# Twelve chunks of a linear attention and a gated feed-forward on one core: d_ff tiles of 512 tokens behind the attention, and filler matmuls in TensorE's planned waits

## The chip, the cores and the metric

The kernel runs on one core of one Trainium2 chip. The metric is the device time of one execution in microseconds. Lower is better.

## The reference

```python
def _attn_ref(r, k, v, w, a, b):            # B=4, H=8, S=768, D=40
    state = zeros(B, H, D, D)
    for t in range(S):
        y[:, :, t] = einsum('bhd,bhde->bhe', rt, state)
        Sa = einsum('bhde,bhe->bhd', state, at)
        state = state * wt[:, :, None, :] - einsum('bhd,bhe->bhde', Sa, bt) + einsum('bhd,bhe->bhde', vt, kt)
def _moe_ref(x, w_a, w_b, w_out):           # x: 3072 x 320, d_ff = 1536
    return ((x @ w_a) * (x @ w_b)) @ w_out
```

The attention's output, with batch and time as 3072 rows and the heads side by side as 320 columns, is the feed-forward's input.

## The kernel before

**Attention.** The 768 steps are cut into 12 chunks of 64 steps (`NS` = 12, `C` = 64). A pair of chunk and batch is numbered q, 48 in all. For each q `prep` scans the decay on VectorE, scales k, a and b, and forms masked 64x64 score blocks on TensorE (`pssc`, `psn`). Per chunk, `lanes` inverts the triangular 32x32 blocks of all heads: the masked blocks go by DMA to DRAM (`nb_d`), come back as one row per block (`N`), 62 small VectorE operations that wait for one another solve them (`Yt`, `psl`), and the results go out (`ts_d`) and back (`TT`) by DMA. `main` then runs the chain of q on TensorE with ScalarE or VectorE between the steps: `psr`, `psu`, `psut`/`psuu`, `psg`, `psy`, `psyt`; `self_state` adds `pss` and `psst`. Each of these ten steps takes one of the four PSUM banks of the attention by `at_take` and gives it back by `at_give`. `values` loads `UV`, `others` loads `rvt`, both on SyncE's queue.

**Feed-forward.** `xform` makes of a chunk's output the operand `xk` (256 tokens; high and low parts of the numbers stand as separate rows, so that 8 products of the list `KT` give one sum). A `Unit` is one tile of 128 d_ff columns for one chunk: 16 matmuls with 256 moving columns into one bank `ab` (two such banks), ScalarE copies one half out, VectorE multiplies it with the other, ScalarE rounds (`gh`), GpSimd takes the rest (`gl`), and 6 matmuls with 320 moving columns add into two banks `po`. There are 12 d_ff tiles and 12 chunks, so 144 units. The first five tiles (`F1`; fewer for the first two chunks, `FIRST`) run among the attention's steps as their chunk comes out, and their sum is kept in DRAM (`po_d`), as is `xk` (`xk_d`). Later tiles come two at a time (`groups`): the first group for chunks 0 and 1 still among the attention, all the rest behind it. A unit that is the last of its job adds `po` into `acc` on VectorE (two operations).

**Order.** All work is written as generators that yield `(engine, inputs, claim, condition)`. `Order.run` keeps a modelled time for each engine and takes, again and again, the step that could start first, `claim` being added to delay it. The program order on each engine is the order so found; the model is used only there. Its numbers are constants: `HOP` and `SPARE` are added to an operand that comes from another engine (`ready`), `LAND` and `PER_KB` price a DMA, and for TensorE it models a clock that halves when the last window of 3.413 us was streamed for less than 0.47 (`issue`). `NWAY`, `LATER`, `WAY`, `SPB`, `AHEAD` delay or permit steps (`after`, `lanes`, `late`). Nearly every DMA is issued by SyncE, in this order.

All instructions are recorded under one line (L178, `Issue.__getattr__`), so the profile is read by tiles.

Of the kernel before, what the change touches and what calls it, by code (L numbers as in the profile page):

```python
# [20 lines left out]
B = 4  # L21
H = 8
D = 40
C = 64
# [13 lines left out]
NI = 2  # L38
NL = 12
WAY = 0.5  # L40
LATER = 2.0
NWAY = 2
URG = 0.05
NEAR = 0.05
FIRST = (2, 3)
AHEAD = 4
SPB = 1
RAW = 2

LIMIT = 2.0 ** 8  # L50


PACE = 42.0
SPARE = 0.4
HOP = 0.1
LAND = 2.1
PER_KB = 0.0046
WINDOW = 3.413

# [8 lines left out]
class Order:  # L68
# [13 lines left out]

    def keys(self, x):
        name = x.name if isinstance(x.name, str) else str(x.name)
        if name.startswith("TT"):
            if any(step == C and n > 1 for step, n in x.ap[1:]):
                return [(name, b) for b in range(B)]
            return [(name, x.offset % (B * H * C) // C % B)]
        return [name]
# [8 lines left out]
    def issue(self, e, op, outs, ins, cost, delay, streamed=0.0):  # L98
        t = self.now[e]
        for x in ins:  # L100
            for k in self.keys(x):
                w, by = self.wrote.get(k, 0.0), self.by.get(k)
                t = max(t, w + (HOP if by != e else 0.0))
        for x in outs:
            for k in self.keys(x):
                if self.by.get(k) != e:
                    t = max(t, self.wrote.get(k, 0.0))
                t = max(t, self.read.get(k, (0.0, e))[0] if self.read.get(k, (0.0, e))[1] != e else 0.0)
        if e in self.port and op not in ("memset", "affine_select") and (e == "gpsimd" or sum(not str(x.name).startswith(("ps", "ab", "po")) for x in ins) > 1):

            t = max(t, self.port["gpsimd" if e == "vector" else "vector"])
            self.port[e] = t + cost
        if e == "tensor":
            w = int(t // WINDOW)
            if w > self.window:
                self.slow = w > self.window + 1 or self.busy < 0.47
                self.window, self.busy = w, 0.0
            self.busy += streamed / WINDOW
            if self.slow:
                cost += streamed  # L120
        elif e == "sync":
# [32 lines left out]
    def run(self):  # L154
        while self.parts:
            best = None
            for p in self.parts:
                e, deps, claim, may = p[1]
                if may is not None and not may():
                    continue  # L160
                t = max([self.now[e]] + [self.ready(x, e) for x in deps])
                t += claim(t) if callable(claim) else claim
                if best is None or t < best[0]:
                    best = (t, p)
            self.step(best[1])


class Issue:
# [18 lines left out]

    def cost(self, op, out, ins, kw):
        n = free(out)
        if self.name == "tensor":  # L190
# [17 lines left out]
        return 0.48, PER_KB * out.shape[0] * n * 4 / 1024  # L208


def token_by_token(tc, p, ps_at, pin, rv, done):
# [79 lines left out]
def wkv_moe(ctx, tc, pin, rv, vn, wa, wb, wo, out):  # L291
# [61 lines left out]
    nb1_d = [dram.tile([B * H, HB, HB], F32, name=f"nb1_d{n}") for n in range(NS)]  # L353
    ts_d = [dram.tile([2, B * H, HB, HB], F32, name=f"ts_d{n}") for n in range(NS)]


    def decode(raw, rows, ncol, dst_hi, dst_lo, claim):

# [77 lines left out]
    class Unit:  # L436
# [8 lines left out]
        def whole(self):  # L445
# [3 lines left out]
            Unit.open += 1  # L449
            Unit.turn.append(self)  # L450
            ab = order.tile(psab, [P, 2, 256], F32, tag="ab", name=f"ab{self.name}", bufs=2)
            for j in range(2):
                for i, (kw, kx) in enumerate(KT):
                    mul(ab[:, j, :], wt[:, j, kw, :], self.xk[:, kx, :], i == 0, i == 7)
                if j == 0:
                    yield "tensor", [], self.claim, None
# [35 lines left out]
            self.ended = True  # L492

        by = "scalar"


    wp = ctx.enter_context(tc.tile_pool(name="wp", bufs=1))
# [60 lines left out]
    def of_batch(x, b):  # L558
# [1 line left out]


    done = types.SimpleNamespace(
        i=0, scan=0, mix=0, free=0, prep=0, lanes=0, merge=0, loads=0, values=0, mask=0, main=0, y=0, state=0, x=0, moe=0, later=0, at=4, tmp=True)

    spare, held = {f"at{i}": None for i in range(4)}, {}

    def at_take(name):

        done.at -= 1
        tag = min(spare, key=lambda x: spare[x] or 0.0)  # L570
        del spare[tag]
        x = order.tile(psa, [P, 512], F32, tag=tag, name=name, bufs=1)
        held[str(x.name)] = tag
        return x

    def at_give(*tiles):
# [88 lines left out]
    def lanes(n):  # L665
        urgent, near = after(URG, n), after(NEAR, n)

        def blocks(hs_of):
            for p0, _, hs in HALVES:
                for j, nb in enumerate((nb0_d[n], nb1_d[n])):  # L670
                    sl = slice(j * HB, (j + 1) * HB)
                    nc.sync.dma_start(
                        out=nb[hs_of(hs)].rearrange("h s t -> s h t"),
                        in_=TT[n % 3][p0 + j * HB:p0 + (j + 1) * HB, hs_of(hs), sl])

# [5 lines left out]
        W = order.tile(pp, [P, 144], F32, tag="Yt", name="Yt", bufs=1)  # L681
        yield "sync", [nb0_d[n], nb1_d[n]], 0.0, None
        for p in range(2):
            nc.sync.dma_start(out=N[p * 64:p * 64 + 32], in_=nb0_d[n])
            nc.sync.dma_start(out=N[p * 64 + 32:p * 64 + 64], in_=nb1_d[n])
# [15 lines left out]
        Y = N[:, 0:HB // 2]  # L701
        nc.scalar.copy(out=Y.rearrange("p i t -> p (i t)"), in_=ps)
        at_give(ps)
        yield "sync", [Y], 0.0, None
        for p in range(2):
            nc.sync.dma_start(
                out=ts_d[n].rearrange("j h (i p) t -> p (j h) i t", p=2)[p], in_=Y[p * 64:(p + 1) * 64])
        done.lanes += 1

# [38 lines left out]

    def values(q):
        n, b = divmod(q, B)  # L750
        yield "sync", [], 0.0, lambda: done.values == q and (q or done.mask) and done.state > q - NU and done.scan > min(q + 2, NS * B - 1)
        done.values += 1
        for p0, hs, _ in HALVES:
            nc.sync.dma_start(out=UV[q % NU][C - p0:2 * C - p0, hs, :], in_=vn[n, b][:, hs])
# [145 lines left out]
    def xform(n):  # L900
        yield "scalar", [], 0.0, lambda: done.y == B * (n + 1) and done.moe >= n - 1
        x = xT_t.pop(n).rearrange("p g b t -> p g (b t)")
        xk = order.tile(mp, [PK, 6, B * C], F32R, tag="xk", name="xk", bufs=2)
        yield from expand(x, xk, nc.gpsimd)
        done.x += 1
        xks[n] = xk
# [1 line left out]
            yield "sync", [xk], 0.05, None  # L908
            nc.sync.dma_start(out=xk_d[n], in_=xk.bitcast(F32))

    acc = {}
    ready_w = set()
    ws1 = [weight_tiles(wp, i) for i in range(F1)]
    sets = [ws1[0:FG], ws1[FG:2 * FG]]
# [21 lines left out]
            return (out[n].rearrange("f p d -> p f d"), acc[n]) if last else None  # L936
        return f

    lp, xk2 = [None], {}

    def all_units():

        def job(n, kk):
            now = FIRST[n] if n < len(FIRST) else F1
            fs = range(now) if kk < 0 else [*range(now, F1), *groups[0]] if kk == 0 else groups[kk]
            last = kk == len(groups) - 1
            for i, f in enumerate(fs):
                yield n, kk, f, i == 0, i == len(fs) - 1, fin1(n) if kk < 0 else fin2(n, last)

        for n in range(NS - 1):  # L950
# [1 line left out]
        for n in range(NE):  # L952
            yield from job(n, 0)
        yield from job(NS - 1, -1)
        for n in (NS - 2, *range(NE, NS - 2), NS - 1):
            yield from job(n, 0)
        for kk in range(1, len(groups)):
            for n in range(NS):
                yield from job(n, kk)

    def moe():
        came = {}
        left = [NS * len(g) for g in groups]
        left[0] += sum(F1 - now for now in FIRST)
        for n, kk, f, first, last, fin in all_units():
            def x_there():
                return n in xks if kk < 0 or n >= NS - 2 else n in xk2
            claim = 0.06
# [31 lines left out]
            ready_w.add(f)  # L1000

    def load_x(pool, n):
        xk2[n] = order.tile(pool, [PK, 6, B * C], F32R, tag=f"xk2_{n}", name=f"xk2_{n}", bufs=1)
        nc.sync.dma_start(out=xk2[n].bitcast(F32), in_=xk_d[n])

    def load_acc(n):
# [162 lines left out]
```

## Time and profile before

| what | value |
|---|---|
| median of 3 runs | 1002.53 us (998.47 to 1003.49) |
| the profiled execution | 997.55 us |
| its span, first to last instruction | 995.8 us |
| TensorE busy, matmuls | 883.7 us (89%) |
| VectorE, ScalarE, GpSimd busy | 601.4, 450.0, 307.6 us |
| mean granted TensorE clock | 0.882 of full |

Tiles name the work: `ab` and `po` are feed-forward, names that begin with `ps` are steps of the attention, `N`, `Yt` and `psl` belong to `lanes`. PE is TensorE's matmul row, SPq the issuing SyncE. In a row of a timeline the columns are start, duration, engine, operation and how many were merged, with the idle time before it in brackets. `PEclk` is the granted clock. In a table of stretches each row has the length, then each engine's busy time with its count of instructions, then clock, DMA share and GB/s.

### The profile page before, as it was taken

What the parts mean: (1) busy time and instruction counts of PE and PEld (TensorE: products, weight loads), DVE (VectorE), ACT (ScalarE), POOL (GpSimd) and SP (SyncE); (2) the same over time, 40 slices, a digit from 0 to 9 for tenths busy, and PEclk for the clock granted to TensorE, in tenths of its full rate; (3) what the DMA queues carried; (4) which work ended last, traced back from release to release, by engine and by line L of the source; (5) the groups of instructions that cost most, each with busy time, mean ns of one, the idle gap of its engine ahead of it and who ended that gap; (6) DMA issues with size and microseconds to landing.
All of it is one profiled execution on the core that took longest, in us unless ns stands there. A gap on an engine that the chain in (4) does not pass through costs nothing.

```text
span 995.8 us, 23157 instructions
## 1 busy us (share of the span) xinstructions
PE 883.7 (89%) x8894; PEld 805.2 (81%) x8894; DVE 601.4 (60%) x1626; ACT 450.0 (45%) x1401; POOL 307.6 (31%) x443
## 2 busy tenths in 40 slices
PE   3146988689897789999999999999999999999997
PEld 3145877678787678888888888788899999999996
DVE  5777465877587847685858584724514648733343
ACT  4153454344555354655555656454533434422221
POOL 2230242323224232323322322213434636622222
PEclk9555677657697669999999999999999999999999
DMA  5452546535647245726555556346469402100013
GB/s 146 98 99 45 119 116 149 124 80 101 157 96 185 32 99 134 151 64 152 134 113 136 114 128 120 87 98 159 122 164 221 98 14 65 32 1 2 1 53 110
DMA packets 132945, 102.53 MB, mean 103 GB/s; under 512 B 86659, under 2 KB 118595, under 8 KB 132827
## 3 DMA queue, kind: packets, MB, share of 16 engines
q1 hardware_dynamic: 132827, 100.98, 43.3%
q8 instruction: 72, 1.18, 0.5%
q14 instruction: 46, 0.38, 0.1%
HBM read 77.03 MB, written 21.94 MB: 99 GB/s over the span
## 4 chain that ended last, share of the span: by engine, by line
PE 63%; DVE 17%; issue 5%; DMA 5%; ACT 4%; POOL 3%; SPq 2%; POOLq 0%; DVEq 0%; ACTq 0%
PE ab L178 23%; PE po L178 11%; PE psr L178 5%; DVE psl L178 5%; DVE Yt L178 4%; PE psg L178 4%; PE pss L178 4%; PE psy L178 3%; PE pssc L178 3%; PE psu L178 3%; SPq L178 2%; DMA N<-nb_d 2%; PE psyt L178 1%; ACT Abd L178 1%; PE psst L178 1%
## 5 line engine op out<-in xcount | busy, mean ns | idle before, releaser
L178 PE MATMUL ab<-xk,wt 120*128 120x256 f32 x2304 | 313.1, 290 | 9.5 <-DMA wt<-wt 3.3
L178 PEld LDWEIGHTS ab<-xk,wt 120*128 120x128 f32 x2304 | 295.6, 195 | 13.3 <-DMA wt<-wt 3.5
L178 POOL TENSOR_TENSOR gl<-asb,gh 128x256 fp32r<-128x256 f32 x144 | 110.9, 772 | 267.2 <-ACT gh L178 266.9
L178 PE MATMUL po<-wo,gh 128*128 128x320 f32 x576 | 157.6, 322 | 10.3 <-ACT gh L178 10.3
L178 DVE TENSOR_TENSOR asb<-ab,asb 128x256 f32<-128x256 f32 x144 | 60.7, 421 | 144.6 <-ACT asb L178 144.2
L178 ACT COPY asb<-ab 128x256 f32<-128x256 f32 x144 | 53.5, 372 | 147.0 <-PE ab L178 146.5
L178 PEld LDWEIGHTS po<-wo,gh 128*128 128x128 f32 x576 | 105.1, 193 | 12.9 <-ACT gh L178 11.7
L178 DVE TENSOR_TENSOR Yt<-psl,N 128x126 f32<-128x126 f32 (+22 forms) x372 | 94.2, 253 | 28.6 <-DMA N<-nb_d 17.3
L178 DVE TENSOR_TENSOR psl<-psl,Yt 128x126 f32<-128x126 f32 (+22 forms) x372 | 97.2, 261 | 11.6
L178 PE MATMUL po<-wo,gl 128*128 128x320 f32 x288 | 93.5, 325 | 5.1 <-POOL gl L178 4.8
L178 PE MATMUL pssc<-Abd,BK 120*128 120x192 f32 (+1 forms) x288 | 68.3, 389 | 30.7 <-ACT Abd L178 18.1
L178 ACT CAST gh<-asb 128x256 fp32r<-128x256 f32 x144 | 58.4, 406 | 75.5 <-DVE asb L178 71.1
L178 PEld LDWEIGHTS pssc<-Abd,BK 120*128 120x128 f32 x288 | 61.8, 247 | 33.3 <-ACT Abd L178 32.5
L178 POOL TENSOR_TENSOR pe<-Pc,rp 120x192 f32<-120x192 f32 x44 | 25.2, 573 | 167.7 <-DVE rp L178 149.5
L178 POOL TENSOR_TENSOR ST<-tmp,pcm 120x360 f32<-120x360 f32 x40 | 34.1, 852 | 100.4 <-DVE tmp L178 100.3
L178 PEld LDWEIGHTS po<-wo,gl 128*128 128x128 f32 x288 | 55.7, 193 | 10.3 <-POOL gl L178 9.7
L178 ACT ACTIVATE Abd<-A,m 120x192 f32<-120x192 f32 x144 | 54.8, 447 | 13.6 <-POOL A L178 11.8
L178 PE MATMUL psg<-rvt 120*128 120x192 f32 (+1 forms) x288 | 58.4, 350 | 0.9 <-DVE tmp L178 0.9
L178 DVE TENSOR_TENSOR acc<-po,acc 128x320 f32<-128x320 f32 x96 | 44.2, 490 | 20.6 <-PE po L178 20.6
L178 PEld LDWEIGHTS psg<-rvt 120*128 120x128 f32 x288 | 53.2, 217 | 2.1 <-DVE tmp L178 1.3
L178 PE MATMUL psr<-UV,TT 64*64 64x40 f32 x768 | 53.6, 254 | 0.5 <-ACT TT L178 0.5
L178 PEld LDWEIGHTS psr<-UV,TT 64*64 64x64 f32 x768 | 42.0, 159 | 14.4 <-issue 8.9
(101 smaller groups left out, 1429.3 us busy)
## 6 DMA issues: line engine op xcount, KB each, us to landing
rvt<-in_rv_dram SPq DMA_DIRECT2D x48, 450.0 KB
I<-in_pin_dram SPq DMA_DIRECT2D x46, 361.9 KB
xk_d<-xk SPq DMA_DIRECT2D x11, 720.0 KB
xk<-xk_d SPq DMA_DIRECT2D x10, 720.0 KB
N<-nb_d SPq DMA_DIRECT2D x48, 128.0 KB
wraw<-in_wa_dram SPq DMA_DIRECT2D x12, 360.0 KB
wraw<-in_wb_dram SPq DMA_DIRECT2D x12, 360.0 KB
wraw<-in_wo_dram SPq DMA_DIRECT2D x12, 320.0 KB
```

The costliest lines, as they stand in the source:

```text
L178: r = fn(*args, **kwargs)
```

## The change

Six things change together.

1. `Pair`: behind the attention (`done.y` and `done.state` complete) one d_ff tile runs for two chunks at once: 16 matmuls with 512 moving columns into two banks, one per half, then one operation each of ScalarE, VectorE, ScalarE and GpSimd over 512 columns, then 12 matmuls with 320 columns into four `po` banks, two of them taken from the attention's four. The last pair of a job adds four banks into two `acc` tiles and issues its two output DMAs after that. Pairs are formed of chunks (2,3) to (8,9) in the first later group and of all twelve chunks in the other groups. For this, `xk` of even and odd chunks lie side by side (`xkr`, `pairs`).
2. `warm`: before an attention step takes its bank, and before a unit takes its `ab` bank, the planner compares the start of the step that it has chosen with the time at which TensorE and the bank are free. If the wait is at least `GAP` (0.8 us), matmuls of the identity with itself (float32, 128 columns) are issued into that bank until no more than `MARGIN` (0.9 us) is left. The step's first matmul overwrites them. Nothing is added from the twelfth finished chunk on (`WARM`).
3. The planner's constants: `SPARE` 0.4 to 1.0, `LAND` 2.1 to 2.4, `NWAY` 2 to 1, `LATER` 2.0 to 1.5, `AHEAD` 4 to 3, `SPB` 1 to 2.
4. `values` waits until the first chunk's `N` loads have been issued (`done.blocks`), with a claim of 0.2 (`VC`). `others` follows `values`, so the `rvt` loads move behind them as well.
5. For the first chunk (`TSQ` = 1) the two `ts_d` writes are issued by ScalarE in place of SyncE. `TWOQ` and `NLQ` are 0 and do nothing.
6. The model of DMA issue covers ScalarE's queue too, and `run` passes the chosen step's start and engine on.

```diff
-LATER = 2.0
-NWAY = 2
+LATER = 1.5
+NWAY = 1
...
-AHEAD = 4
-SPB = 1
+AHEAD = 3
+SPB = 2
+GAP = 0.8
+MARGIN = 0.9
+TWOQ = 0
+TSQ = 1
+NLQ = 0
+VC = 0.2
+WARM = 12
...
-SPARE = 0.4
+SPARE = 1.0
-LAND = 2.1
+LAND = 2.4
...
+    def warm(ps):
+        if order.turn != "tensor" or done.x >= WARM:
+            return
+        t = max(order.now["tensor"], order.wrote.get(order.keys(ps)[0], 0.0))
+        if order.start - t < GAP:
+            return
+        while order.start - order.now["tensor"] > MARGIN:
+            mul(ps[:, 0:P], ident, ident)
...
             ab = order.tile(psab, [P, 2, 256], F32, tag="ab", name=f"ab{self.name}", bufs=2)
+            warm(ab.rearrange("p j t -> p (j t)"))
...
+    class Pair(Unit):
...
+        def whole(self):
+            wt, wot = self.w
+            yield "tensor", [self.xk, wt], self.claim, lambda: Unit.open < 3 and (
+                done.at + Unit.ab_free - 2 * (len(Unit.po or ()) < 4) >= 2)
...
+            ab = [self.take(f"{self.name}_{j}") for j in range(2)]
+            for j in range(2):
+                for i, (kw, kx) in enumerate(KT):
+                    mul(ab[j][0].rearrange("p (c t) -> p c t", c=2), wt[:, j, kw, :], self.xk[:, :, kx, :], i == 0, i == 7)
...
+            nc.scalar.copy(out=g, in_=ab[0][0])
...
+            nc.vector.tensor_mul(out=g, in0=ab[1][0], in1=g)
...
+            nc.scalar.copy(out=gh, in_=g)
...
+            nc.gpsimd.tensor_sub(out=gl, in0=g, in1=gh.bitcast(F32))
...
+            for hf in range(4):
+                sl = slice(hf * P, (hf + 1) * P)
+                po = Unit.po[hf][:, :DM]
+                mul(po, gh[:, sl], wot[:, 0, :], self.is_first, False)
+                mul(po, gl[:, sl], wot[:, 0, :], False, False)
+                mul(po, gh[:, sl], wot[:, 1, :], False, self.is_last)
...
         x = order.tile(psa, [P, 512], F32, tag=tag, name=name, bufs=1)
         held[str(x.name)] = tag
+        warm(x)
...
-        yield "sync", [Y], 0.0, None
+        eng = nc.scalar if n < TSQ else nc.sync
+        yield "scalar" if n < TSQ else "sync", [Y], 0.0, None
         for p in range(2):
-            nc.sync.dma_start(
+            eng.dma_start(
...
-        yield "sync", [], 0.0, lambda: done.values == q and (q or done.mask) and done.state > q - NU and done.scan > min(q + 2, NS * B - 1)
+        yield "sync", [], VC, lambda: done.values == q and done.blocks and done.state > q - NU and done.scan > min(q + 2, NS * B - 1)
...
-        for n in (NS - 2, *range(NE, NS - 2), NS - 1):
-            yield from job(n, 0)
+        yield from job(NS - 2, 0)
+        for n in range(NE, NS - 2, 2):
+            yield from job((n, n + 1), 0)
+        yield from job(NS - 1, 0)
         for kk in range(1, len(groups)):
-            for n in range(NS):
-                yield from job(n, kk)
+            for n in range(0, NS, 2):
+                yield from job((n, n + 1), kk)
```

More of the change, by code (lines that the diff above doesn't have):

```diff
@@ L84, in keys @@
         name = x.name if isinstance(x.name, str) else str(x.name)
+        if name.startswith("xkr"):
+            return [(name, x.offset % (12 * B * C) // (6 * B * C))] if len(x.shape) < 4 else [(name, 0), (name, 1)]
         if name.startswith("TT"):
@@ L108, in issue @@
                 t = max(t, self.read.get(k, (0.0, e))[0] if self.read.get(k, (0.0, e))[1] != e else 0.0)
+        if op == "dma_start":
+            streamed = 0.0
         if e in self.port and op not in ("memset", "affine_select") and (e == "gpsimd" or sum(not str(x.name).startswith(("ps", "ab", "po")) for x in ins) > 1):
@@ L120, in issue @@
                 cost += streamed
-        elif e == "sync":
+        elif op == "dma_start":
             self.moved = max(self.moved, t) + delay
@@ L160, in run @@
                     continue
-                t = max([self.now[e]] + [self.ready(x, e) for x in deps])
-                t += claim(t) if callable(claim) else claim
+                at = max([self.now[e]] + [self.ready(x, e) for x in deps])
+                t = at + (claim(at) if callable(claim) else claim)
                 if best is None or t < best[0]:
-                    best = (t, p)
+                    best = (t, p, at, e)
+            self.start, self.turn = best[2:]
             self.step(best[1])
@@ L189, in cost @@
         n = free(out)
+        if op == "dma_start":
+            return 0.48, PER_KB * out.shape[0] * n * 4 / 1024
         if self.name == "tensor":
@@ L207, in cost @@
             return (0.1 + 0.0005 * n if op in ("memset", "affine_select") else 0.33 + 0.0016 * n), 0.0
-        return 0.48, PER_KB * out.shape[0] * n * 4 / 1024
 def token_by_token(tc, p, ps_at, pin, rv, done):
@@ L494, in wkv_moe, with take, give @@
         by = "scalar"
+    class Pair(Unit):
+        @staticmethod
+        def take(name):
+            if Unit.ab_free:
+                Unit.ab_free -= 1
+                return order.tile(psab, [P, 2, 256], F32, tag="ab", name=f"ab{name}", bufs=2).rearrange("p j t -> p (j t)"), True
+            return at_take(f"ps{name}"), False
+        @staticmethod
+        def give(ps, own):
+            if own:
+                Unit.ab_free += 1
+            else:
+                at_give(ps)
+        def whole(self):
+            wt, wot = self.w
+            yield "tensor", [self.xk, wt], self.claim, lambda: Unit.open < 3 and (
+                done.at + Unit.ab_free - 2 * (len(Unit.po or ()) < 4) >= 2)
+            Unit.open += 1
+            Unit.turn.append(self)
+            ab = [self.take(f"{self.name}_{j}") for j in range(2)]
+            for j in range(2):
+                for i, (kw, kx) in enumerate(KT):
+                    mul(ab[j][0].rearrange("p (c t) -> p c t", c=2), wt[:, j, kw, :], self.xk[:, :, kx, :], i == 0, i == 7)
+                if j == 0:
+                    yield "tensor", [], self.claim, None
+            self.begun = True
+            yield "scalar", [ab[0][0]], 0.0, None
+            g = order.tile(self.pool, [P, 512], F32, tag="asb2", name="asb2", bufs=2)
+            nc.scalar.copy(out=g, in_=ab[0][0])
+            self.give(*ab[0])
+            yield "vector", [g], 0.0, None
+            nc.vector.tensor_mul(out=g, in0=ab[1][0], in1=g)
+            self.give(*ab[1])
+            yield "scalar", [g], 0.0, lambda: self in (Unit.turn[0], Unit.turn[min(1, len(Unit.turn) - 1)])
+            gh = order.tile(self.pool, [P, 512], F32R, tag="gh2", name="gh2", bufs=2)
+            nc.scalar.copy(out=gh, in_=g)
+            yield "gpsimd", [gh], 0.0, None
+            gl = order.tile(self.pool, [P, 512], F32R, tag="gl2", name="gl2", bufs=2)
+            nc.gpsimd.tensor_sub(out=gl, in0=g, in1=gh.bitcast(F32))
+            yield "tensor", [gl, wot], self.claim, lambda: Unit.turn[0] is self and (not self.is_first or Unit.po_free and done.at > 1)
+            if self.is_first:
+                Unit.po_free = False
+                Unit.po = [order.tile(pso, [P, 512], F32, tag="po", name=f"po{self.name}_{hf}", bufs=2) for hf in range(2)]
+                Unit.po += [at_take(f"ps{self.name}_{hf}") for hf in range(2)]
+            for hf in range(4):
[4 more added lines that the diff above has]
+                mul(po, gh[:, sl], wot[:, 1, :], False, self.is_last)
+                if hf < 3:
+                    yield "tensor", [], self.claim, None
+            Unit.turn.popleft()
+            Unit.open -= 1
+            if self.is_last:
+                po, then = Unit.po, []
+                for i in range(2):
+                    yield "vector", po[2 * i:2 * i + 2], 0.0, None
+                    then.append(self.done[i](po[2 * i:2 * i + 2]))
+                at_give(*po[2:])
+                Unit.po_free, Unit.po = True, None
+                for x in then:
+                    if x:
+                        nc.sync.dma_start(out=x[0], in_=x[1])
+            self.ended = True
@@ L562, in wkv_moe @@
     done = types.SimpleNamespace(
-        i=0, scan=0, mix=0, free=0, prep=0, lanes=0, merge=0, loads=0, values=0, mask=0, main=0, y=0, state=0, x=0, moe=0, later=0, at=4, tmp=True)
+        blocks=0, i=0, scan=0, mix=0, free=0, prep=0, lanes=0, merge=0, loads=0, values=0, mask=0, main=0, y=0, state=0, x=0, moe=0, later=0, at=4, tmp=True)
     spare, held = {f"at{i}": None for i in range(4)}, {}
@@ L671, in blocks @@
                     sl = slice(j * HB, (j + 1) * HB)
-                    nc.sync.dma_start(
+                    (nc.scalar if j and n < TWOQ else nc.sync).dma_start(
                         out=nb[hs_of(hs)].rearrange("h s t -> s h t"),
@@ L683, in lanes @@
         for p in range(2):
-            nc.sync.dma_start(out=N[p * 64:p * 64 + 32], in_=nb0_d[n])
-            nc.sync.dma_start(out=N[p * 64 + 32:p * 64 + 64], in_=nb1_d[n])
+            (nc.scalar if p and n < NLQ else nc.sync).dma_start(out=N[p * 64:p * 64 + 32], in_=nb0_d[n])
+            (nc.scalar if p and n < NLQ else nc.sync).dma_start(out=N[p * 64 + 32:p * 64 + 64], in_=nb1_d[n])
+        done.blocks += 1
         yield "scalar", [nb0_d[n], nb1_d[n]], 0.0, lambda: done.at > SPB
@@ L703, in lanes @@
         at_give(ps)
-        yield "sync", [Y], 0.0, None
+        eng = nc.scalar if n < TSQ else nc.sync
+        yield "scalar" if n < TSQ else "sync", [Y], 0.0, None
         for p in range(2):
-            nc.sync.dma_start(
+            eng.dma_start(
                 out=ts_d[n].rearrange("j h (i p) t -> p (j h) i t", p=2)[p], in_=Y[p * 64:(p + 1) * 64])
@@ L902, in xform @@
         x = xT_t.pop(n).rearrange("p g b t -> p g (b t)")
-        xk = order.tile(mp, [PK, 6, B * C], F32R, tag="xk", name="xk", bufs=2)
+        if n == 0:
+            xkr.append(order.tile(mp, [PK, 2, 6, B * C], F32R, tag="xkr", name="xkr", bufs=1))
+        xk = xkr[0][:, n % 2]
         yield from expand(x, xk, nc.gpsimd)
@@ L909, in xform @@
             nc.sync.dma_start(out=xk_d[n], in_=xk.bitcast(F32))
-    acc = {}
+    acc, xkr = {}, []
     ready_w = set()
@@ L937, in fin2 @@
         return f
-    lp, xk2 = [None], {}
+    lp, xk2, pairs = [None], {}, {}
     def all_units():
         def job(n, kk):
-            now = FIRST[n] if n < len(FIRST) else F1
+            now = FIRST[n] if not isinstance(n, tuple) and n < len(FIRST) else F1
             fs = range(now) if kk < 0 else [*range(now, F1), *groups[0]] if kk == 0 else groups[kk]
@@ L947, in job @@
             for i, f in enumerate(fs):
+                if isinstance(n, tuple):
+                    yield n, kk, f, i == 0, i == len(fs) - 1, [fin2(x, last) for x in n]
+                    continue
                 yield n, kk, f, i == 0, i == len(fs) - 1, fin1(n) if kk < 0 else fin2(n, last)
@@ L965, in moe, with there @@
         for n, kk, f, first, last, fin in all_units():
+            if isinstance(n, tuple):
+                def there():
+                    return all(x in acc and (x >= NS - 2 or x in xk2) for x in n)
+                yield "tensor", [], 0.06, lambda: there() and f in ready_w and done.y == NS * B and done.state == NS * B and (
+                    Unit.open < 3 and done.at + Unit.ab_free - 2 * (len(Unit.po or ()) < 4) >= 2)
+                x = pairs[n[0] // 2] if n[0] < NS - 2 else xkr[0]
+                u = Pair(lp[0], f"{n[0]}_{f}", x, dest(f), first, last, fin, 0.06)
+                order.part(u.whole())
+                while not u.begun:
+                    yield "tensor", [], 0.0, lambda: u.begun
+                done.later += 2
+                left[kk] -= 2
+                finished.update({kk} if left[kk] == 0 else ())
+                continue
             def x_there():
@@ L1002, in load_x @@
     def load_x(pool, n):
-        xk2[n] = order.tile(pool, [PK, 6, B * C], F32R, tag=f"xk2_{n}", name=f"xk2_{n}", bufs=1)
+        if n // 2 not in pairs:
+            pairs[n // 2] = order.tile(pool, [PK, 2, 6, B * C], F32R, tag=f"xk2_{n}", name=f"xk2_{n}", bufs=1)
+        xk2[n] = pairs[n // 2][:, n % 2]
         nc.sync.dma_start(out=xk2[n].bitcast(F32), in_=xk_d[n])
```

## The prediction

> **What bounds the kernel now.** I read the page first, then a table of stretches, then what TensorE waits for, then timelines.
>
> ```profile
> span 995.8 us, 23157 instructions
> ...
> PE 883.7 (89%) x8894; PEld 805.2 (81%) x8894; DVE 601.4 (60%) x1626; ACT 450.0 (45%) x1401; POOL 307.6 (31%) x443
> ...
> PE   3146988689897789999999999999999999999997
> ...
> PEclk9555677657697669999999999999999999999999
> ```
>
> TensorE is the bound, but from slice 2 to slice 15 of the 40 it is busy on a clock that is well below full. The table of stretches, cut where that changes:
>
> ```profile
> 36.30:114.80 78.50, 44.31 (x403) 38.55 (x404) 56.15 (x175) 25.55 (x85) 9.42 (x18) 0.50 0.41 83
> 114.80:377.60 262.80, 226.75 (x2240) 195.98 (x2239) 179.53 (x504) 130.12 (x425) 81.10 (x117) 0.72 0.48 111
> 377.60:723.00 345.40, 335.96 (x4148) 297.04 (x4148) 220.38 (x635) 191.35 (x628) 102.18 (x148) 1.00 0.54 123
> 723.00:988.00 265.00, 261.61 (x2054) 260.04 (x2052) 124.44 (x264) 88.71 (x222) 103.59 (x126) 1.00 0.26 69
> ```
>
> First a stage with much idle time at clock 0.50, then one that is 86% busy at 0.72, then 97% and 99% at full clock. So the end is set by TensorE's work, plus its idle time, plus what the low clock adds. What the low clock adds: the same step of the attention in a slow and in a fast stretch (columns: group and count, then busy us and mean ns of one).
>
> ```profile
> L178 PE MATMUL psu<-RH,TT 64*64 64x40 f32 x32 | 2.6, 307 | 0.0
> ```
> ```profile
> L178 PE MATMUL psu<-RH,TT 64*64 64x40 f32 x96 | 4.6, 229 | 0.0
> ```
>
> 2.6/32 = 81 ns (204 to 224 us) against 4.6/96 = 48 ns (480 to 560 us): 1.7 times. A feed-forward tile goes from 120 to 224 ns a matmul (rows below), 1.87 times. With 1.75, a busy slow microsecond holds 0.43 us of loss. At clock 0.72 about 56% of a stretch is at half clock: 0.56 x 226.75 x 0.43 = 55 us between 115 and 378, and 44.31 x 0.43 = 19 us between 36 and 115.
>
> What lowers the clock (smaller stretches):
>
> ```profile
> 200.10:203.60 3.50, 0.57 (x3) 0.60 (x4) 3.43 (x7) 2.04 (x5) 2.77 (x4) 0.99 0.17 26
> ...
> 207.00:224.00 17.00, 16.73 (x145) 14.19 (x145) 13.05 (x47) 5.96 (x27) 0.79 (x1) 0.50 0.29 63
> ...
> 149.30:152.40 3.10, 0.91 (x9) 0.60 (x7) 0.70 (x2) 2.54 (x7) 0.49 (x1) 0.99 0.60 160
> 152.40:166.00 13.60, 12.96 (x81) 10.76 (x82) 5.18 (x15) 4.58 (x15) 3.94 (x5) 0.50 0.77 190
> ```
>
> Twice a wait of 2 to 3 us at full clock is followed by 14 to 17 us at half clock, though TensorE is then busy 95% and more. So a short wait costs far more than itself: 13.6 or 17 us x 0.43 = 6 to 7 us. The Trainium skill (TensorE: Matmul & The Clock Gate, the table of what to do in "Why this matters for your kernels") asks only that no gap be longer than about 3 us. By that rule the 2.2 us idle at 149 to 152 would be harmless and filling it would gain nothing; the trace disagrees there.
>
> **The change, part by part.**
>
> *Fillers from 115 to 378 us.* TensorE's waits (total us, times, longest), from 115 to 390:
>
> ```profile
> PE po L178 <- ACT gh L178: 8.6, 4, 3.5
> PE psuu L178 <- DVE rp L178: 4.7, 1, 4.7
> PE ab L178 <- DMA wt<-wt: 3.3, 1, 3.3
> PE pssc L178 <- DVE BK L178: 3.1, 1, 3.1
> PE pssc L178 <- ACT Abd L178: 2.8, 1, 2.8
> ...
> PE ab L178 <- POOL xk L178: 1.5, 1, 1.5
> PE ab L178 <- ACT xk L178: 1.5, 1, 1.5
> ```
>
> A filler can stand only ahead of a step that takes a bank of the attention or an `ab` bank. That covers 4.7 + 3.3 + 3.1 + 2.8 + 1.5 + 1.5 = 16.9 us of these 25.5 and not the 8.6 before `po`: two thirds. It covers them only where the planner foresees them; I take half of the 55 us, **-28**, with ends 0 and -55. The waits themselves stay; fillers take their place.
>
> *Fillers from 36 to 115 us.*
>
> ```profile
> 54.69 0.86 PE L178 MATMUL psn<-ident,BK 120*128 120x120 f32 x3 [21.05 <-DVE TT L178]
> 60.73 3.78 PE L178 MATMUL pssc<-Abd,BK 120*128 120x192 f32 x12 [5.18 <-ACT Abd L178]
> ...
> 88.97 0.36 PE L178 MATMUL psuu<-ident,UV 64*120 64x64 f32 x1 [5.91 <-DVE ST L178]
> ```
>
> All three waits precede bank-taking steps. VectorE's 62 dependent steps of `lanes` set the pace up to about 89 us, so a faster TensorE gains only behind them, where it is nearly always busy: about 24 us x 0.43 = 10. I take **-8**, ends 0 and -19.
>
> *Pairs.* 4 pairs of chunks x 2 tiles, then 6 x 5: 38 pairs, in place of 76 of the 144 units. Columns streamed and `po` matmuls stay the same; a pair saves 16 matmul starts.
>
> ```profile
> 906.87 2.08 PE L178 MATMUL ab<-xk,wt 120*128 120x256 f32 x16
> 908.79 0.31 PE L178 MATMUL po<-wo,gh 128*128 128x320 f32 x1
> ...
> 909.67 2.08 PE L178 MATMUL ab<-xk,wt 120*128 120x256 f32 x16
> ```
> ```profile
> 220.11 3.78 PE L178 MATMUL ab<-xk,wt 120*128 120x256 f32 x16
> ...
> 223.69 2.09 PE L178 MATMUL psg<-rvt 120*128 120x192 f32 x12
> ```
>
> Starts: (908.79 - 906.87)/16 = 120 ns for 256 columns, (909.67 - 908.79)/6 = 147 ns for 320: 0.42 ns a column and 13 ns a matmul. The half-clock row gives (223.69 - 220.11)/16 = 224 ns; if only the streaming doubles, that is 104 + 16. So 16 x 13 ns x 38 = **-8**, ends -7 and -10. The Trainium skill (same page, "Back-to-back issue gap") gives columns/2.4 + 2.5 ns for one start; by that the pairs would save 1.5 us and the sum below would be 6.5 us less. Its 109 ns for 256 columns is not the 120 that the trace has.
>
> Does the chain behind a pair fit? Operations of 512 columns that stand in the trace:
>
> ```profile
> L178 DVE TENSOR_TENSOR acc<-po,acc 128x320 f32<-128x320 f32 x96 | 44.2, 490 | 20.6 <-PE po L178 20.6
> L178 DVE TENSOR_TENSOR G<-psg,tri 128x512 f32<-128x512 f32 x48 | 33.0, 689 | 22.4 <-PE psg L178 21.8
> ...
> L178 POOL TENSOR_TENSOR xk<-xT,xk 120x512 fp32r<-120x512 f32 x12 | 15.4, 1282 | 0.0
> ...
> L178 ACT CAST xk<-xT 120x512 fp32r<-120x512 f32 x12 | 7.4, 620 | 5.5 <-DVE xT L178 4.1 <-PE ab L178 1.4
> ```
>
> After the second half: 0.69 + 0.62 + 1.28 = 2.6 us, under the next pair's 32 half-starts, 16 x 0.227 = 3.6 us. The four additions at a job's end, 4 x 0.49 = 2.0 us on VectorE, also fit under them, so they cost nothing; without that cover each of the 4 + 18 jobs would lose up to 2 us, +44. At the very end nothing covers: two more additions (+1.0) and a second 320 KB output in flight.
>
> ```profile
> 740.00:760.00 20.00, 20.00 (x160) 20.00 (x159) 5.69 (x14) 6.36 (x17) 5.18 (x7) 1.00 0.99 230
> ```
>
> At the 230 GB/s of that stretch, 0.33 MB is 1.4 us. The first pair needs x and `acc` of two chunks (2 x 1.06 MB) where one unit needed one: up to +4.6 us at that rate, of which units in between hide most, +1. Pairs: -8 + 2.5 + 1 = **-4.5**.
>
> *SyncE's queue at the start.*
>
> ```profile
> 22.45 6.27 SPq L178 DMA_DIRECT2D nb_d<-TT  x8
> 28.77 2.42 SPq L178 DMA_DIRECT2D UV<-in_vn_dram  x4
> 31.29 1.92 SPq L178 DMA_DIRECT2D N<-nb_d  x4
> ...
> 54.66 1.79 SPq L178 DMA_DIRECT2D nb_d<-TT  x4
> 56.55 1.31 SPq L178 DMA_DIRECT2D ts_d<-N  x2
> ```
>
> `UV` moves behind `N`: 2.4 us, or less if `N` then waits for the last `nb_d` to land. `ts_d` no longer stands behind four `nb_d` issues: 1.8 us; ScalarE pays 1.3 us of issue, with copies for the next chunk queued behind it. Together -4.2, ends 0 (if the second chunk's `lanes` sets the pace anyway) and -6; **-4**. `UV` and `rvt` come later, but TensorE first needs them after 70 us.
>
> *What the fillers and the spare cost.* A filler ends up to 0.9 us before a planned start that already holds 1.1 us of spare and hop, so where the plan is exact it ends 0.2 us late; where the operand comes sooner than planned, more. No row shows it. With 21 foreseen waits it is 21 x 0.2 = 4, with three times as many 13; below nothing only if the new order happens to be better. **+6**, ends 0 and +20. `SPB` lets the copy into `psl` start only with three banks free, which holds back the 62 steps of `lanes` by a step of the attention at most; `NWAY` and `LATER` take half a microsecond off claims; `AHEAD` loads one `acc` later. All taken at 0, within these ends.
>
> Sum: -28 - 8 - 4.5 - 4 + 6 = **-38.5**. Span 995.8 - 38.5 = 957; with the 1.75 us around it (997.55) 959. The median of the runs shown, 1002.53, is 5.0 above that execution: **964**.
>
> **Rivals.** *The gate still closes.* The waits before `po` stay, and any one of them costs 14 to 20 us of half clock, so the stretch may fall back each time; the 95% busy slow rows show that work alone doesn't bring the clock back. Then -4.5 - 4 + 2 = -6.5: 996. Against it: of the five longest kinds of wait all but one can be filled. The skill's rule on gaps would come out near here too, since it leaves only the waits of more than 3 us worth filling. *The gate stays open throughout.* -55 - 19 - 4.5 - 4 + 6 = -76: 926. For it: 345 us at clock 1.00 after 378, with the same steps. *Slower: fillers for waits that don't come.* With 1.1 us of spare on each operand from another engine the planner sees waits of 0.8 us where none are. By the `pssc` row above (six float32 products in 3.78 us, each two records, 171 columns on average) a filler of 128 columns takes about 0.47 us at half clock and 0.24 at full, say 0.3. 48 x 10 steps take a bank. With no gain from the gate, pairs and start give 994, and from 28 false fillers on (8.5/0.3) all is lost; 100 give 1024. With the forecast's 36 us from the gate it takes 150. Against it: attention steps are interleaved with feed-forward work, which the planner puts into a wait first.
>
> **How the numbers follow.** The forecast 0.58, gate closed 0.17, gate open 0.15, slower 0.10. About 0.5% (5 us) is what a measurement of this kernel can tell from no change. Slower takes its 0.10; same takes half of the gate-closed case, 0.08; faster the rest, 0.82. The forecast's own range is 945 to 985 (fillers -10 to -45). The range reaches down into the open-gate case and up over the closed-gate one: 932 to 1000.
>
> **What would show it.** PEclk 9 from slice 5 on in place of slice 16; matmuls of the identity into attention banks; 608 `ab` matmuls with 512 columns, about 227 ns apart, and 1088 with 256; the `N` loads issued near 28 us; the attention's end moved from 723 to about 690; the stretch behind it 4 to 8 us shorter up to the last `po`. It is wrong if the clock row keeps its fives and sixes, or if idle time before attention steps grows by more than the low clock gave back.

## The result, and the profile after

| | us |
|---|---|
| before, median of 4 runs beside it | 1000.5 (995.11 to 1003.49) |
| changed, median of 4 runs | 959.54 (957.36 to 963.8) |
| ratio, with its 95% interval | 0.9602 (0.9545 to 0.9658) |
| the profiled execution of the changed kernel | 963.80, span 961.6, clock 0.964 |

The forecast was 964, so the sum came out. The experiments below show that two of its terms were wrong and that they cancelled. First the page of the changed kernel, the lines that answer to those of before:

```profile
span 961.6 us, 23562 instructions
...
PE 927.0 (96%) x9230; PEld 833.0 (87%) x9230; DVE 586.5 (61%) x1588; ACT 436.8 (45%) x1325; POOL 299.5 (31%) x405
...
PE   9999998999897999999999999999999999999996
...
PEclk9999989599995999999999999999999999999999
```

The clock row is nearly all nines, and TensorE is busy from the first slice on. This looks much like what the prediction said would show it. The stretches of the changed kernel (the attention, read at the end of its last `xT`, now ends at 695.5 us in place of 721.1):

```profile
0.00:114.80 114.80, 111.53 (x1147) 107.51 (x1148) 83.06 (x240) 49.37 (x161) 26.78 (x65) 1.00 0.54 121
114.80:350.00 235.20, 217.01 (x2472) 190.51 (x2472) 170.47 (x475) 120.76 (x391) 73.35 (x105) 0.88 0.54 122
350.00:690.00 340.00, 334.39 (x4098) 298.20 (x4097) 215.50 (x633) 186.71 (x617) 97.96 (x141) 0.99 0.51 118
697.50:954.00 256.50, 255.48 (x1445) 229.03 (x1444) 110.45 (x225) 76.11 (x146) 97.56 (x91) 1.00 0.27 70
```

The busy time of the first two rows holds the fillers. The two largest groups of them (matmul records, busy us, mean ns):

```profile
L190 PE MATMUL pssc<-ident 128*128 128x128 f32 x548 | 65.1, 280 | 1.4 <-POOL ident masks.py:199 1.4
...
L190 PE MATMUL ab<-ident 128*128 128x128 f32 x198 | 22.6, 275 | 0.0
```

There are 944 such records in all. SyncE's queue at the start, and ScalarE's issue of the first `ts_d`:

```profile
19.80 3.65 SPq L190 DMA_DIRECT2D nb_d<-TT  x8
24.14 1.72 SPq L190 DMA_DIRECT2D N<-nb_d  x4
```
```profile
48.08 0.59 ACT L190 COPY N<-psl 128x512 f32<-128x512 f32 x1 [17.20 <-issue]
48.69 1.33 ACTq L190 DMA_DIRECT2D ts_d<-N  x2
```

The `N` loads go out at 24.1 us in place of 31.3, and the first `ts_d` at 48.7 in place of 56.6. A pair behind the attention:

```profile
940.89 3.90 PE L190 MATMUL ab<-xk,wt 120*128 120x512 f32 x16
944.63 0.31 PE L190 MATMUL po<-wo,gh 128*128 128x320 f32 x1
...
946.39 3.90 PE L190 MATMUL ab<-xkr,wt 120*128 120x512 f32 x16
```

16 starts take 944.63 - 940.89 = 3.74 us, 234 ns each, and the twelve `po` matmuls 1.76 us. Six of the twelve write banks that are named `ps`, since they come from the attention's four. The last such matmul, before and after:

```profile
989.14 0.30 PE L178 MATMUL po<-wo,gh 128*128 128x320 f32 x1
```
```profile
954.73 0.31 PE L190 MATMUL ps<-wo,gh 128*128 128x320 f32 x1
```

### The profile page after: what moved, and what is told of

Same layout as the page of the kernel before. It is cut to its first block, busy times and chain, and to the rows that moved or that the text cites. A ratio compares the mean times of both kernels' runs of the same rounds, so it can differ in the third digit from the quotient of the medians.

```text
span 961.6 us, 23562 instructions
## 1 busy us (share of the span) xinstructions
PE 927.0 (96%) x9230; PEld 833.0 (87%) x9230; DVE 586.5 (61%) x1588; ACT 436.8 (45%) x1325; POOL 299.5 (31%) x405
## 4 chain that ended last, share of the span: by engine, by line
PE 73%; DVE 11%; DMA 5%; SPq 3%; issue 3%; POOL 3%; ACT 2%; DVEq 0%; POOLq 0%
PE ab L190 26%; PE po L190 9%; PE pssc L190 8%; PE psr L190 5%; PE psy L190 5%; PE psg L190 4%; PE ps L190 4%; SPq L190 3%; DVE psl L190 3%; DVE Yt L190 3%; PE pss L190 3%; PE psu L190 2%; DMA I<-in_pin_dram 2%; PE psw L190 2%; PE pst L190 2%
## 5 line engine op out<-in xcount | busy, mean ns | idle before, releaser
L190 POOL TENSOR_TENSOR gl<-asb,gh 128x256 fp32r<-128x256 f32 (+1 forms) x106 | 103.0, 972 | 253.7 <-ACT gh L190 241.6
L190 PE MATMUL ab<-xkr,wt 120*128 120x256 f32 (+1 forms) x1024 | 149.5, 298 | 0.0
L190 DVE TENSOR_TENSOR asb<-ab,asb 128x256 f32<-128x256 f32 (+1 forms) x104 | 53.3, 513 | 149.5 <-PE ab L190 88.9
L190 PE MATMUL ab<-xk,wt 120*128 120x512 f32 (+1 forms) x656 | 142.1, 368 | 0.0
L190 PEld LDWEIGHTS ab<-xkr,wt 120*128 120x128 f32 x1024 | 133.6, 192 | 4.9
L190 PEld LDWEIGHTS ab<-xk,wt 120*128 120x128 f32 x656 | 112.7, 188 | 19.1
L190 ACT CAST gh<-asb 128x256 fp32r<-128x256 f32 (+1 forms) x106 | 51.3, 484 | 110.2 <-DVE asb L190 109.0
L190 ACT COPY asb<-ab 128x256 f32<-128x256 f32 (+1 forms) x106 | 47.7, 450 | 106.3 <-PE ab L190 104.9
L190 PE MATMUL pssc<-ident 128*128 128x128 f32 x548 | 65.1, 280 | 1.4 <-POOL ident masks.py:199 1.4
L190 PEld LDWEIGHTS pssc<-ident 128*128 128x128 f32 x548 | 63.7, 196 | 1.6 <-POOL ident masks.py:199 1.4
```

Source lines behind the costliest of these rows:

```text
L190: r = fn(*args, **kwargs)
```

## The experiments

How far the attention had come is read from the operation that ends a q, VectorE's `xT`: its count in a table of stretches, in brackets after the first busy time. Before, to 115, to 350 and to 690 us:

```profile
0.00:115.00 115.00, 1.06 (x3) 0.00 (x0) 0.00 (x0) 0.63 0.47 104
115.00:350.00 235.00, 4.58 (x13) 4.93 (x12) 7.79 (x8) 0.74 0.50 114
350.00:690.00 340.00, 9.81 (x28) 8.62 (x21) 13.87 (x14) 0.96 0.53 120
```

The changed kernel:

```profile
0.00:115.00 115.00, 1.43 (x4) 1.23 (x3) 1.95 (x2) 1.00 0.54 121
115.00:350.00 235.00, 5.57 (x16) 3.69 (x9) 5.86 (x6) 0.88 0.54 122
350.00:690.00 340.00, 9.21 (x26) 8.63 (x21) 13.76 (x14) 0.99 0.51 118
```

By 350 us 20 of the 48 q are done in place of 16, with the same 54 `po` matmuls (9 units) in both. The lead of the attention is made there: from 350 to 690 us the changed kernel does two q fewer and 30 `po` matmuls (5 units) more, 234 against 204.

**Pairs alone.**

```diff
 # the changed kernel, with what differs from before except Pair taken back
+LATER = 2.0; NWAY = 2; AHEAD = 4; SPB = 1; SPARE = 0.4; LAND = 2.1
+TSQ = 0; VC = 0.0; WARM = 0
+        yield "sync", [], VC, lambda: done.values == q and (q or done.mask) and done.state > q - NU and ...
```

> The kernel before with pairs alone: no fillers, the planner's constants and the queues at the start as before. Theory (the gate of TensorE's clock is the main gain, pairs a term of their own): 7 to 10 us faster than before, ratio 0.990 to 0.993, all of it behind the attention; clock digits as before. Rival (pairs lose at the loads and at the tail what they save in matmul starts): ratio 0.997 or more.

Ratio 0.9932 (0.9899 to 0.9964), median 992.6 against 999.12. The attention ends where it did, at 720.5 us, and from there to the end of the last matmul of a `po` sum it is 261.4 us in place of 268.3. The theory holds, at the lower end of its size. By 350 us this kernel has done 18 q, two more than before, and its attention ends no earlier for it: a count at one instant is no finer than that.

**Single units in place of pairs, the rest kept.**

```diff
+        for n in range(NE, NS - 2):
+            yield from job(n, 0)
...
+            for n in range(NS):
+                yield from job(n, kk)
```

> The changed kernel with single units in place of pairs. Theory: the pairs' 8 to 10 us are lost and nothing else, ratio to before 0.967 to 0.970, clock as in the changed kernel (0.96 to 0.97). Rival (pairs are worth nothing): 0.960.

0.9703 (0.9661 to 0.9744) against 0.9602 with pairs: 1.0%. Both ways around, pairs are worth 0.7 to 1.0%. The traces put the loss where the theory has it: the attention ends at 698.1 us in place of 695.5, and behind it the time to the end of the last matmul of a `po` sum is 270.2 us in place of 259.5.

**No fillers, planned without them.**

```diff
+WARM = 0
```

> The changed kernel without fillers (WARM = 0), everything else kept. Theory (fillers hold the clock): mean granted clock falls back to about 0.88, and 28 to 36 us of the gain are lost: ratio to the kernel before 0.985 to 1.0. Rival (the planner's new constants, above all SPARE, order the work better, and the fillers ride along): ratio 0.972 or less, with the clock well above 0.90.

0.9802 (0.9757 to 0.9847), clock 0.897. It lies between the two expectations. Half of the gain is lost with the fillers, but the planner also made another order once it priced none. The runs with the order held fast, below, take the two apart.

**Fillers alone, on the kernel before.** As in the first experiment, but with `WARM` = 12 and single units.

> The kernel before with fillers alone: old constants (SPARE 0.4), old queues at the start, single units. Theory (the gate is the gain, and the fillers hold it whatever the constants): ratio 0.965 to 0.975, clock 0.95 or more. Rival (with little spare the planner foresees too few waits, and the fillers hold the gate only together with SPARE 1.0): ratio 0.985 or more, clock below 0.93.

Slower than before: 1.0112 (1.0072 to 1.0152), though the clock rose to 0.950. Its `xT` counts:

```profile
0.00:115.00 115.00, 1.43 (x4) 1.23 (x3) 1.95 (x2) 0.88 0.42 101
115.00:350.00 235.00, 5.57 (x16) 3.69 (x9) 6.11 (x6) 0.93 0.56 128
350.00:690.00 340.00, 8.35 (x24) 8.62 (x21) 13.80 (x14) 0.95 0.46 105
```

At 350 us it is as far as the changed kernel, and then it does 24 q where the changed one does 26 and the kernel before 28. The feed-forward falls behind as well; `po` matmuls in that stretch, here and in the changed kernel:

```profile
350.00:690.00 340.00, 38.52 (x198) 29.70 (x198) 0.00 (x0) 5.54 (x14) 0.95 0.46 105
```
```profile
350.00:690.00 340.00, 46.53 (x234) 35.55 (x234) 0.00 (x0) 6.51 (x16) 0.99 0.51 118
```

TensorE, fillers included, is idle there for 21 of the 340 us, and for 6 in the changed kernel. A better clock did not make a faster kernel. This broke the theory as it stood, and half of the rival with it: the fillers held the clock with old constants.

**The same order with thin fillers.** The plan is the same, instruction by instruction, but each filler streams one column.

```diff
-            mul(ps[:, 0:P], ident, ident)
+            tc.keep_in_program_order(nc0.tensor.matmul(ps[:, 0:1], lhsT=ident, rhs=ident[:, 0:1], start=True, stop=True))
+            order.issue("tensor", "matmul", [ps[:, 0:P]], [ident], 2 * P / 1200 + 0.01, 0.2, P / 600)
```

> The changed kernel with the same program order, in which each filler streams 1 column in place of 128 (same weights loaded, same count, priced the same in the plan). Theory (fillers work by keeping the array streaming, so that the clock stays up): clock 0.90 or less, ratio to before 0.985 to 1.02, at least 20 us above the changed kernel. Rival (what gains is the order that the planner makes when it believes in a full clock): clock may fall, but ratio 0.97 or less.

1.0685 (1.0646 to 1.0725), far beyond both expectations. The test did not isolate what it was meant to, for a filler became longer, not shorter:

```profile
L377 PE MATMUL pssc<-ident 128*128 128x1 f32 x548 | 113.6, 343 | 1.4 <-POOL ident masks.py:199 1.4
L377 PE MATMUL ab<-ident 128*128 128x1 f32 x198 | 38.6, 331 | 0.0
```
```profile
0.00:114.80 114.80, 113.36 (x542) 113.28 (x542) 49.41 (x141) 23.64 (x74) 16.99 (x46) 1.00 0.31 72
114.80:350.00 235.20, 230.03 (x2055) 210.69 (x2056) 134.24 (x403) 93.65 (x308) 47.41 (x75) 0.69 0.40 89
```

113.6/548 = 207 ns a record, against 65.1/548 = 119 with 128 columns. TensorE is full throughout the first 115 us at clock 1.00, and VectorE gets 49.4 us of work done there in place of 83.1. So fillers that outlast the wait hold everything up, even at full clock.

**SPARE back to 0.4.**

> The changed kernel with SPARE = 0.4 in place of 1.0. Theory (with little spare the plan lets TensorE wait for operands that it believes to be there, and no filler covers that; this is why fillers alone made the kernel before slower): ratio 0.985 to 1.01, clock near 0.95, more TensorE idle time than in the changed kernel. Rival (NWAY, LATER, SPB or the start made the difference between fillers alone and the changed kernel): ratio 0.970 or less.

0.9709 (0.9672 to 0.9745). The theory that spare is what fillers need falls; the middle value is within 0.1% of the rival's bound.

**Fillers up to the first chunk only (WARM = 1).**

> The changed kernel with fillers up to the first finished chunk only (WARM = 1). Theory (the first chunk's lead is lost to the second chunk's lanes, which VectorE paces; the gain of the fillers comes from the waits between 115 and 350 us): ratio 0.975 to 0.982, near the kernel without fillers. Rival (the start is where fillers gain): ratio 0.966 or less.

Six runs from 971.87 to 996.90 us, median 988.76, with no ratio. Even the fastest is 0.972 of the median beside it (1000.3), above the rival's bound, so the rival falls by its own number. Whether the theory holds can't be said: five of the six lie at 987.82 us or more, above its range, and the order changed with the fillers.

**The start's queues as before.**

```diff
+TSQ = 0; VC = 0.0
+        yield "sync", [], VC, lambda: done.values == q and (q or done.mask) and done.state > q - NU and ...
```

> The changed kernel with the start's queues as before: UV and rvt loads not held back for the N loads, ts_d of the first chunk issued by SyncE. Theory: 2 to 4 us slower than the changed kernel, ratio 0.962 to 0.965. Rival (the second chunk's lanes set the pace at the start whatever the first does): no difference, 0.960.

0.9880 (0.9841 to 0.9919), 28 us of the gain, against 2 to 4 expected. Its `xT` counts, and then those of the changed kernel, at another cut:

```profile
0.00:115.00 115.00, 1.42 (x4) 1.24 (x3) 1.97 (x2) 0.96 0.49 108
115.00:412.00 297.00, 7.01 (x20) 6.13 (x15) 9.84 (x10) 0.93 0.52 122
412.00:690.00 278.00, 7.09 (x20) 6.16 (x15) 9.84 (x10) 0.93 0.49 114
```
```profile
0.00:115.00 115.00, 1.43 (x4) 1.23 (x3) 1.95 (x2) 1.00 0.54 121
115.00:412.00 297.00, 6.99 (x20) 6.16 (x15) 8.27 (x9) 0.90 0.52 118
412.00:690.00 278.00, 7.79 (x22) 6.17 (x15) 11.36 (x12) 0.99 0.52 120
```

Their `po` matmuls up to the same cut, old start first:

```profile
0.00:412.00 412.00, 20.11 (x90) 15.02 (x90) 0.00 (x0) 3.20 (x8) 0.93 0.51 118
```
```profile
0.00:412.00 412.00, 21.70 (x102) 16.06 (x102) 0.00 (x0) 3.13 (x8) 0.93 0.52 119
```

At 412 us both have done 24 q, and the old start is 12 `po` matmuls (2 units) behind. By the starts in the prediction's rows a unit is 16 x 120 + 6 x 147 ns = 2.8 us of TensorE, so that is an estimated 6 us. Most of the 28 us is lost after that, more than 350 us behind the loads at the start. What the edit still changes there is the claim of 0.2 us on each `UV` load (`VC`) and the order that the planner found.

**The same order without fillers.** Fillers are priced in the plan but not issued. This kernel, the next one and the one with thin fillers have the changed kernel's plan, step by step.

```diff
-            mul(ps[:, 0:P], ident, ident)
+            order.issue("tensor", "matmul", [ps[:, 0:P]], [ident, ident], 2 * P / 1200 + 0.01, 0.2, P / 600)
```

> The changed kernel in exactly its planned order, the fillers priced in the plan but not issued. It separates the fillers from the order that the planner makes with them. Theory (fillers hold the clock, and that is most of the gain): clock about 0.90, ratio to before 0.985 to 1.01, 25 us or more above the changed kernel. Rival (the order makes the gain): ratio 0.972 or less.

0.9682 (0.9637 to 0.9726): the rival. Its profiled span is 961.1 us, that of the changed kernel 961.6; these are its second fastest execution of six and the other's slowest of four, and the medians, 966.46 and 959.54, are 7 us apart. Stretches, then `xT` counts:

```profile
0.00:114.80 114.80, 60.77 (x514) 53.94 (x514) 81.86 (x239) 48.68 (x160) 26.51 (x65) 0.70 0.52 120
114.80:350.00 235.20, 200.03 (x2211) 172.73 (x2212) 170.94 (x477) 120.78 (x393) 73.67 (x105) 0.80 0.54 122
350.00:690.00 340.00, 333.91 (x4064) 296.94 (x4063) 216.97 (x635) 186.45 (x617) 98.26 (x142) 0.98 0.51 118
```
```profile
0.00:115.00 115.00, 1.42 (x4) 1.23 (x3) 1.94 (x2) 0.70 0.52 120
115.00:350.00 235.00, 5.57 (x16) 3.69 (x9) 5.87 (x6) 0.80 0.54 122
350.00:690.00 340.00, 9.20 (x26) 8.63 (x21) 13.71 (x14) 0.98 0.51 118
```

The clock is 0.70 and 0.80 in place of 1.00 and 0.88, and the q come out in the same numbers: 4, 16, 26. TensorE is idle for 54 us in the first stretch and 35 in the second (3 and 18 with fillers). Its slower matmuls stretched into time in which it would otherwise have waited. VectorE's work in those stretches is the same within 1.5%.

**The same order, fillers in long waits only.**

```diff
+        long = order.start - t >= 3.4
         while order.start - order.now["tensor"] > MARGIN:
+            if long:
+                mul(ps[:, 0:P], ident, ident)
+                continue
+            order.issue("tensor", "matmul", [ps[:, 0:P]], [ident, ident], 2 * P / 1200 + 0.01, 0.2, P / 600)
```

> The same planned order, fillers issued only where the planned wait is 3.4 us or more. Theory (a wait of 1 to 3 us is enough to close the gate): between the two, ratio 0.970 to 0.990, clock 0.91 to 0.95. Rival (only waits above about 3 us close the gate, as the Trainium skill's TensorE: Matmul & The Clock Gate says): ratio 0.958 to 0.965, clock 0.96 or more.

0.9603 (0.9556 to 0.9651), as with all fillers. So by the middle values fillers are worth about 0.8% in this order, and those in the short waits nothing that shows. The time is as the rival has it, and so as the Trainium skill's rule (TensorE: Matmul & The Clock Gate, "Why this matters for your kernels") would have it. The clock is not as the rival has it: 0.938 to 0.957 in the six executions, nearer to the theory's range, against 0.964 to 0.974 with all fillers. Leaving the short waits empty lowered the clock and did not cost time.

From one execution of the same kernel to the next, though, the time does go with the clock. The runs with fillers in long waits only took 951.47 us at clock 0.957 and 963.27 at 0.945; the changed kernel took 957.36 at 0.974 and 963.80 at 0.964; the kernel before, in the runs beside the first experiments, 992.65 at 0.886 and 1006.52 at 0.870. That is 6 to 10 us for 0.01 of clock. With the order held and the fillers taken out, the clock falls from about 0.97 to about 0.90 and the medians differ by 7 us in all. So that slope does not say what a better clock is worth. Which comes first within a kernel, the longer wait or the lower clock, no run here shows.

**Two touches without a meaning: SPARE = 1.01, and LAND = 2.41.**

> The changed kernel with SPARE = 1.01 in place of 1.0: nothing that a mechanism could feel, but the planner's ties fall otherwise. Theory (the planner's order is sensitive, and the 28 us that the queues at the start were worth are for the most part such a change of order): 5 us or more away from the changed kernel, ratio 0.965 to 0.990. Rival (sizes are smooth): ratio 0.957 to 0.963.

> The changed kernel with LAND = 2.41 in place of 2.4, a second such touch. Theory: again 5 us or more away, ratio 0.965 to 0.990. Rival: ratio 0.957 to 0.963.

0.9700 (0.9657 to 0.9743) and 0.9684 (0.9633 to 0.9735), against 0.9602: by the middle values 8 to 10 us slower, with intervals that overlap. A change of the order that nobody intends may be worth about 1%; the overlap leaves that short of shown. Two of the single edits above that change the order went clearly beyond it: no fillers (0.9802) and the start's queues (0.9880).

## Why the prediction was right in its sum and wrong in its terms

- **The step that failed: "So the end is set by TensorE's work, plus its idle time, plus what the low clock adds."** The loss from the low clock is real as TensorE's time, but up to 350 us, where it mostly falls, little of it is time of the kernel. Where TensorE waits a little later for VectorE, a DMA or ScalarE, a slow matmul only uses up the wait. The two terms -28 and -8 for the fillers measure 0 to about -8 together (0.9682 to 0.9602, intervals that overlap), fillers' own cost included. This is shown in the changed kernel's order; no run gives the kernel before a better clock in its own order, since fillers alone changed that too. The sign that I read past: the stretch at clock 0.72 was busy 86%, the one before it 56%. A stage with that much idle time is paced by something else, and a slow clock there is a mark of waiting before it is a cause.
- **"All taken at 0, within these ends"** was the other error. The order that the planner makes with the new constants, the new queues and its belief in fillers is worth 0.9932 - 0.9682 = 2.5%, about 25 us, the largest part of the gain. With the -4 for the queues that was short by about 21 us, and the fillers' -30 net was too much by about 22. That the two cancelled is chance.
- **Pairs, -4.5.** Measured -7 to -10. A start of 512 columns takes 234 ns, not 227, so the starts save only 16 x 6 ns x 38 = 4 us. Stalls gave the rest in part: before, TensorE was idle for 3.4 of 265 us there, after for 1.0 of 256.5. From the attention's end to the end of the last matmul of a `po` sum it is 268.3 against 259.5 us; some 3 us of that I can't place. The chain of a pair fits under the next one, as argued. The tail cost 0.2 us in place of 2.5 (6.4 us from that matmul to the end before, 6.6 after), and the wait for the first pair's data did not come.
- **The start's queues, -4.** Locally -7 (`N` loads) to -8 us (`ts_d`). Whether that reached the end can't be said: against the run with the old start the fourth q ends 14.8 us sooner (93.0 and 107.8), the eighth 1.2 us (169.5 and 170.7), most of the 28 us of the experiment was lost behind 412 us, and the order changed with the edit.
- **The rivals.** "The gate still closes" was priced at 996. With the gate closed in the same order it is 966 (0.9682). "Slower" happened with longer fillers (1.0685), by the mechanism named, TensorE occupied when its operand is there. It also happened where fillers stood alone (1.0112), but there TensorE was idle for longer from 350 us on, so the order is the likelier cause; no run separates the two.
- **The rule weighed there.** The trace still shows that a short wait lets the clock fall, and the run with fillers in long waits only bears it out (clock 0.938 to 0.957). Filling the short waits as well gained no time, as by the rule. But I put the rule's outcome near 996, and filling the long waits alone gave 960.

What stays open: which property of the order makes it better. The changed order does four more q by 350 us, and so do fillers alone, which lose that lead later; no run here shows which decision of the planner that hangs on, since every edit moves many.

## What to carry to other kernels

Price a slow clock only where the engine is the last to be waited for. A stretch at half clock that is also full of waits may give nothing back. And when a kernel's order comes from a planner, hold the order fast to test one of its effects, and touch a constant by 1% or less to see what an order by itself is worth, before a gain is put down to the edit that caused it.

## What the runs showed of the hardware

- A float32 matmul of 128 x 128 weights with 1 moving column took 207 ns a record in the fillers, one with 128 columns 119 ns. Why the shorter one takes longer is not settled.
- With one-column fillers nearly back to back (438 of the 542 matmul records, 93.8 of the first 114.8 us) the granted clock stayed at 1.00. So it was held there with few streamed columns.
- Matmuls of 512 columns started 234 ns apart, of 256 columns 120, of 320 columns 147.
